# Block B's projection: weight parts from copies in PSUM, x's sums begun in block A, loads ahead of V moved

## The chip, the cores and the metric

The kernel runs on one core of one Trainium2 chip. A core has a matrix engine (PE), which multiplies and adds up in PSUM, eight banks of 128 partitions by 512 numbers; a vector engine (DVE) and an activation engine (ACT), which read and write PSUM and the on-chip memory SBUF; a general engine (POOL), which this kernel uses on SBUF alone; and SyncE (SP), whose queue issues the transfers (DMAs) here. The metric is the device time of one execution in microseconds (us), less is better. Each engine works through its own queue in program order.

## The reference

Two attention blocks of the same sizes, whose results stand side by side in the output: 2048 positions, width 640, 32 heads of 20.

```python
qkv = (x @ wqkv).reshape(B, S, 3, H, Dh)            # both blocks
# block A: each position attends to 8 positions, 2 apart (masked before 0)
logits = einsum("bhsd,bhswd->bhsw", q, kg) * scale
o = einsum("bhsw,bhswd->bhsd", softmax(logits), vg)
# block B: full attention
scores = einsum("bhqd,bhkd->bhqk", q, k) * Dh ** -0.5
o = einsum("bhqk,bhkd->bhqd", softmax(scores), v)
out = concatenate([oA @ woA, oB @ woB], axis=-1)
```

## The kernel before, in words

**Products in parts.** Every fp32 operand is split into a high part (`act.copy` to a rounded type) and a low part (raw minus high, `lo_of`, a `tensor_tensor` subtraction on DVE). A product of 128 rows by 512 columns over one block of 128 takes three matmuls (`PASSES`: high by high, high by low, low by high).

**Stages.** First block A's q, k, v projection for 12 of 16 row tiles (`a_steps`, line 825, driven by the loop at line 862, steps n = 0 to 47). Then block B's q and k projection, 40 groups g0 to g39 (`groups_b`, line 1059, driven by the loop at line 1076). Then block B's v projection, the V stage (line 1664), in groups too, with the first maxima of block B's scores beside it from the seventh group on. Then the attention loop, 512 steps for block B with block A's rest beside it, and the output products.

**Block B's groups.** The 1280 columns of q and k go by ten chunks of 128, taken in pairs, five `WFour` objects WF0 to WF4 (line 768); x goes by four column blocks n of 512. For n = 3 and 2 a pair is multiplied plainly (`b_plain`, line 1048: four groups of 15 matmuls). For n = 0 and 1 the pair and the two blocks of x are multiplied as a two by two scheme with seven products in place of eight (`b_four`, line 1015: four groups of 27, 15, 9 and 3 matmuls). It needs sums of weight blocks (`WFour.sums`) and of x blocks (`XFour.sums`, line 714), and the high and low parts of both: `base` makes the parts of the blocks as they are, `second` those of the sums. The order is: plain WF0 (g0 to g3), plain WF1 (g4 to g7), fours WF0 (g8 to g11) and WF1 (g12 to g15), plain WF2, four WF2, plain WF3, four WF3, four WF4, plain WF4 (g36 to g39). The k columns come first in that order, the q columns after.

**Order of the work.** It is written out by hand. After each group the table `jobs` (line 1067) adds loads, parts and sums to the queues. x's sums run on POOL; WF0's and WF1's weight sums on POOL, the others on DVE; all in place in SBUF. A group's result is evicted by `b_parts` (line 1004): ACT writes the high part into an SBUF tile `pr` from a ring of three, and the low part is put off: `low` (line 999), called in a later group, subtracts on DVE and issues the store on SP. Banks are taken in turn from all eight (`next_bank`, line 446). Block A's attention runs on POOL from g9 on: `a_fetch` (line 537) loads a unit's keys or values into one of two buffers `akv`, and a step of `a_attention` (line 639) is a unit of POOL work. `b_keys` and `b_queries` (lines 969 and 979) load K and q of the first head group for the maxima; `wide_pieces` (line 220) loads v's weights and puts their parts off by `wait[0]` ticks, a tick being a group. A tile taken from a ring waits for all users of its predecessor in that place. Most instructions are recorded by a helper at line 61 (`InOrder`), so the profile gives that line for all of them, and they are told apart by tile: `w` weight parts, `xn`, `xs` and `xl` x's parts, `stg` raw loads, `pr` outputs, `ps_st` PSUM, `bk` and `bq` K and q for attention, `akv` block A's keys and values.

## Time and profile before

| | |
|---|---|
| median of 3 runs | 1759.67 us (1758.86 to 1764.15) |
| the profiled execution | 1763.64 us, span 1761.8 us |
| busy share of the span | PE 98%, DVE 86%, ACT 77%, POOL 72% |
| block B's projection | 147.5 to 298.5 us |
| V stage to the loop | 298.5 to 400.5 us |

A row of the timeline gives the start and the length of a run of like instructions in us, the engine, the operation, output and inputs by tile, their shape and count, and in brackets how long the engine idled before and what ended that. A row of the groups gives total and mean time, then the idle time. A row of the stretches gives the length, each engine's busy time and count (PE, PEld for weight loads, DVE, ACT, POOL; PE alone where only PE was asked for), then the clock granted to PE, the share of DMA time and GB/s.

### The profile page before, as it was taken

What the parts mean: (1) busy time and instruction counts of PE and PEld (TensorE: products, weight loads), DVE (VectorE), ACT (ScalarE), POOL (GpSimd) and SP (SyncE); (2) the same over time, 40 slices, a digit from 0 to 9 for tenths busy, and PEclk for the clock granted to TensorE, in tenths of its full rate; (3) what the DMA queues carried; (4) which work ended last, traced back from release to release, by engine and by line L of the source; (5) the groups of instructions that cost most, each with busy time, mean ns of one, the idle gap of its engine ahead of it and who ended that gap; (6) DMA issues with size and microseconds to landing.
All of it is one profiled execution on the core that took longest, in us unless ns stands there. A gap on an engine that the chain in (4) does not pass through costs nothing.

```text
span 1761.8 us, 32264 instructions
## 1 busy us (share of the span) xinstructions
PE 1731.3 (98%) x11193; PEld 980.3 (56%) x11193; DVE 1517.2 (86%) x2110; ACT 1350.4 (77%) x2639; POOL 1270.7 (72%) x1154
## 2 busy tenths in 40 slices
PE   9999899899999999999999999999999999999999
PEld 8887678775444444444444444445444444444458
DVE  7757574589999999999999999999999999999656
ACT  5224233118999899999999999998999999989882
POOL 0003687395888888888998888988888988868324
PEclk9999899999999999999999999999999999999999
DMA  7667578784445563644464446535553534231223
GB/s 238 221 203 253 199 269 276 223 262 115 142 133 150 138 173 117 165 150 130 139 172 150 139 130 163 161 115 157 136 177 98 137 108 131 80 106 46 58 79 116
DMA packets 224411, 271.20 MB, mean 154 GB/s; under 512 B 92908, under 2 KB 147448, under 8 KB 224248
## 3 DMA queue, kind: packets, MB, share of 16 engines
q1 hardware_dynamic: 223672, 268.49, 51.7%
q8 instruction: 88, 1.44, 0.4%
q14 instruction: 75, 0.61, 0.1%
q10 hardware_dynamic: 576, 0.66, 0.1%
HBM read 194.31 MB, written 74.74 MB: 153 GB/s over the span
## 4 chain that ended last, share of the span: by engine, by line
PE 87%; DVE 4%; DMA 3%; POOL 2%; ACT 1%; issue 1%; SPq 0%; DVEq 0%; POOLq 0%; ACTq 0%
PE ps_st L61 87%; DVE mx L61 2%; DMA bk<-kb_d 1%; ACT e L61 1%; DMA stg<-wqk_b 1%; DVE stg L61 1%; POOL xo L61 1%; DVE w L61 1%; DMA stg<-wv_b 0%; POOL braw L61 0%; POOL xr L61 0%; DMA wr<-xa 0%; POOL stg L61 0%; DMA stg<-xb 0%; SPq L61 0%
## 5 line engine op out<-in xcount | busy, mean ns | idle before, releaser
L61 DVE TENSOR_REDUCE mx<-ps_st 128x1 f32<-128x512 f32 (+1 forms) x1500 | 1218.3, 879 | 79.8 <-PE ps_st L61 68.7
L61 ACT ACTIVATE e<-ps_st 128x512 f32<-128x512 f32 x2048 | 1067.2, 609 | 45.6 <-PE ps_st L61 24.4
L61 PE MATMUL ps_st<-bq,bk 62*128 62x512 f32 x2048 | 612.8, 439 | 0.2
L61 PE MATMUL ps_st<-bk,bq 60*128 60x512 f32 x2048 | 558.1, 435 | 7.2 <-DMA bq<-qb_d 6.0
L61 PEld LDWEIGHTS ps_st<-bq,bk 62*128 62x128 f32 x2048 | 287.4, 184 | 480.6 <-ACT e L61 337.4
L61 PE MATMUL ps_st<-e,vb 128*32 128x512 f32 x4096 | 542.9, 604 | 2.0
L61 POOL TENSOR_TENSOR braw<-braw,more 128x512 f32<-128x512 f32 x224 | 287.7, 1284 | 127.5 <-ACT more L61 119.8
L61 POOL TENSOR_TENSOR akv<-akv 128x640 f32<-128x640 f32 (+3 forms) x304 | 283.4, 932 | 23.8
L61 PEld LDWEIGHTS ps_st<-bk,bq 60*128 60x128 f32 x2048 | 265.7, 184 | 40.6 <-DVE mx L61 12.0
L61 POOL TENSOR_TENSOR akv<-akv,aq 128x1280 f32<-128x1280 f32 x64 | 188.5, 2945 | 28.0 <-DMA akv<-ka_d 28.0
L61 PEld LDWEIGHTS ps_st<-e,vb 128*32 128x32 f32 x4096 | 82.0, 108 | 156.2 <-issue 71.1
L61 POOL TENSOR_TENSOR akv<-akv,al 128x1280 f32<-128x1280 f32 x64 | 151.6, 2369 | 2.3 <-DMA akv<-va_d 2.2
L61 POOL TENSOR_TENSOR stg<-stg 128x512 f32<-128x512 f32 (+1 forms) x16 | 21.1, 1320 | 161.0 <-DVE xs L61 156.8
L61 PE MATMUL ps_st<-wc,xn 128*128 128x512 f32 (+1 forms) x544 | 133.4, 377 | 0.1
L61 ACT COPY more<-ps_st 128x512 f32<-128x512 f32 x224 | 132.5, 591 | 0.7 <-PE ps_st L61 0.4
L61 ACT COPY ro<-ps_st 128x320 f32<-128x320 f32 (+2 forms) x76 | 34.7, 460 | 106.0 <-PE ps_st L61 80.8
L61 PEld LDWEIGHTS ps_st<-wc,xn 128*128 128x128 f32 x544 | 102.1, 188 | 15.1 <-ACT xn L61 0.5
L61 PE MATMUL ps_st<-xn,w 128*128 128x512 f32 x360 | 92.0, 404 | 8.8 <-DVE ps_st L61 4.3
L61 PEld LDWEIGHTS ps_st<-xn,w 128*128 128x128 f32 x360 | 70.2, 196 | 25.4 <-DVE ps_st L61 4.7
L61 ACT CAST pr<-ps_st 128x512 fp32r<-128x512 f32 x40 | 23.4, 587 | 76.3 <-PE ps_st L61 52.0
L61 PE MATMUL ps_st<-ww,aot 128*128 128x320 f32 x480 | 77.8, 314 | 1.7
L61 POOL TENSOR_TENSOR ao<-ao,akv 128x640 f32<-128x640 f32 x48 | 74.8, 1558 | 3.8
(116 smaller groups left out, 1393.3 us busy)
## 6 DMA issues: line engine op xcount, KB each, us to landing
akv<-ka_d SPq DMA_DIRECT2D x128, 320.0 KB
akv<-va_d SPq DMA_DIRECT2D x128, 320.0 KB
wx<-wa_d SPq DMA_DIRECT2D x24, 480.0 KB
kb_d<-pr SPq DMA_DIRECT2D x20, 512.0 KB
qb_d<-pr SPq DMA_DIRECT2D x20, 512.0 KB
bk<-kb_d SPq DMA_DIRECT2D x16, 640.0 KB
bq<-qb_d SPq DMA_DIRECT2D x64, 160.0 KB
rb<-s_d SPq DMA_DIRECT2D x128, 64.0 KB
```

The costliest lines, as they stand in the source:

```text
L61: return self.tc.keep_in_program_order(op(*a, **k))
```

## The change

Block B's weight parts and sums take their operands from PSUM: `lift` lets ACT copy the raw weight blocks into two banks, DVE's sums have one operand there and write their results c and d to banks, and the high and low parts are made from them. WF0 keeps its first parts as they were (`base(False)`). WF0's and WF1's sums leave POOL for DVE. Two or three banks are kept for this (`block_of`), so the groups no longer turn through all eight: g0 takes bank 6, g1 to g7 turn through 0, 1, 2, and from g8 on five banks, 0 to 4, are dealt out by `order_b`. The parts of the last x blocks (`ends`) are subtracted on POOL. Of x's first pair the end parts and half of its sums are made in the last step of block A, and WF1's loads go out in the step before; the rest of x's sums and parts is spread otherwise over jobs 0 to 6. Every fourth output goes to a pair of tiles of another tag (`rb`), stored by two DMAs. v's weight pieces, K's and q's loads are issued earlier; two of block A's fetches move behind g39 to V groups 3 and 5.

```diff
@@ -718,39 +718,46 @@
...
-        def parts(self, hi, lo, src):
+        def parts(self, hi, lo, src, e=dve):
             act.copy(hi, src)
-            lo_of(lo, src, hi)
+            e.tensor_tensor(lo, src, hi.bitcast(F32), ALU.subtract)
+
+        def ends_of(self, kp):
+            self.e.append([p_tile([128, 2, 512], F32R, "xs", "px") for _ in range(3)] if kp else
+                          [sb.tile([128, 2, 512], F32R, tag=tag, bufs=b, name="xs")
+                           for tag, b in (("aot", 1), ("akx", 2), ("akx", 2))])
+            e = self.e[kp][0]
+            self.parts(e[:, 0], e[:, 1], self.raw[kp][1][:, 1])
...
                 self.u = [big(n, [128, 2, KC - 1, 512], "xn") for n in range(2)]
-                self.e.append([sb.tile([128, 2, 512], F32R, tag=tag, bufs=b, name="xs")
-                               for tag, b in (("aot", 1), ("akx", 2), ("akx", 2))])
-            else:
-                self.e.append([p_tile([128, 2, 512], F32R, "xs", "px") for _ in range(3)])
-            u, e = self.u[0][:, :, 2 * kp:2 * kp + 2], self.e[kp][0]
+            u = self.u[0][:, :, 2 * kp:2 * kp + 2]
             self.parts(u[:, 0], u[:, 1], self.raw[kp][0])
-            self.parts(e[:, 0], e[:, 1], self.raw[kp][1][:, 1])
...
                 t = sb.tile([128, 2, 512], F32R, tag="last0", bufs=2, name="xl")
-                self.parts(t[:, 0], t[:, 1], r)
+                self.parts(t[:, 0], t[:, 1], r, gp)
                 self.l.append(lambda i, t=t: t[:, i])
-        def sums(self, kp):
+        def sums(self, kp, part):
             a, b = self.raw[kp]
-            pool(b[:, 1], b[:, 1], b[:, 0], ALU.subtract)
-            pool(b[:, 0], b[:, 0], a[:, 0], ALU.subtract)
+            if not part:
+                pool(b[:, 1], b[:, 1], b[:, 0], ALU.subtract)
+                pool(b[:, 0], b[:, 0], a[:, 0], ALU.subtract)
+                return
             pool(a[:, 0], b[:, 1], a[:, 0], ALU.add)
...
             self.parts(u[:, 0], u[:, 1], self.raw[kp][0])
-            for n in range(2):
+            for n in range(2 - kp):
                 self.parts(e[n + 1][:, 0], e[n + 1][:, 1], self.raw[kp][1][:, n])
+
+        def third(self):
+            self.parts(self.e[1][2][:, 0], self.e[1][2][:, 1], self.raw[1][1][:, 1])
...
@@ -769,7 +776,7 @@
...
         def __init__(self, m, tag, bufs):
-            self.m = MS[2 * m:2 * m + 2]
+            self.n, self.m = m, MS[2 * m:2 * m + 2]
             self.raw = [sb.tile([128, KC, 128], F32, tag=tag, bufs=bufs, name="stg") for _ in range(2)]
...
@@ -779,26 +786,53 @@
...
-        def base(self):
+        def block_of(self, n):
+            r = ((3, 4, 4, 5), (6, 7, 4, 5), (6, 7, 5, 5))[min(self.n, 2)][n]
+            return bank_b(r).rearrange("p (k c) -> p k c", c=128)
+
+        def lift(self):
+
+            self.s = [self.block_of(n) for n in range(2)]
+            for t, r in zip(self.s, self.raw):
+                act.copy(t, r[:, :KC - 1])
+
+        def base(self, lift=True):
             self.x, self.y = (sb.tile([128, 2, KC + 1, 128], F32R, tag="w", bufs=4, name="w") for _ in range(2))
             a, b = self.raw
-            self.parts(self.x, 0, a)
-            self.parts(self.y, 0, b[:, :KC - 1])
-            self.parts(self.x, KC, b[:, KC - 1:])
-
-        def sums(self, e):
-            a, b = ([t[:, o:KC - 1:2] for o in range(2)] for t in self.raw)
-            e.tensor_tensor(b[1], b[0], b[1], ALU.add)
-            e.tensor_tensor(b[0], a[0], b[0], ALU.subtract)
-            e.tensor_tensor(a[0], b[1], a[0], ALU.subtract)
-            e.tensor_tensor(a[1], a[1], a[0], ALU.subtract)
+            if not lift:
+                self.parts(self.x, 0, a)
+                self.parts(self.y, 0, b[:, :KC - 1])
+                self.parts(self.x, KC, b[:, KC - 1:])
+                return
+            self.lift()
+            t = self.block_of(2)[:, :2]
+            for o in range(2):
+                act.copy(t[:, o:o + 1], self.raw[o][:, KC - 1:])
+            self.lows = [(self.x[:, :, :KC - 1], self.s[0]), (self.y[:, :, :KC - 1], self.s[1]), (self.x[:, :, KC - 1:], t)]
+            for u, t in self.lows:
+                act.copy(u[:, 0], t)
+
+        def lo(self):
+            for u, t in self.lows:
+                lo_of(u[:, 1], t, u[:, 0])
+
+        def sums(self):
+            (A, B), (a, b) = self.s, self.raw
+            c, d = self.block_of(3), A
+            ev, od = slice(0, KC - 1, 2), slice(1, KC - 1, 2)
+            for r, x, y, op in ((c[:, od], B[:, ev], b[:, od], ALU.add), (c[:, ev], A[:, ev], b[:, ev], ALU.subtract),
+                                (d[:, ev], c[:, od], a[:, ev], ALU.subtract), (d[:, od], a[:, od], d[:, ev], ALU.subtract)):
+                dve.tensor_tensor(r, x, y, op)
+            self.c, self.d = c, d
         def second(self):
-            a, b = self.raw
             self.z = sb.tile([128, 2, KC + 1, 128], F32R, tag="vb", bufs=2, name="w")
-            self.parts(self.z, 0, a[:, :KC - 1])
-            self.parts(self.y, KC - 1, b[:, :2])
-            self.parts(self.z, KC - 1, b[:, 2:KC - 1])
+            uses = ((self.z, 0, self.d), (self.y, KC - 1, self.c[:, :2]), (self.z, KC - 1, self.c[:, 2:]))
+            uses = [(u[:, :, k:k + t.shape[1]], t) for u, k, t in uses]
+            for u, t in uses:
+                act.copy(u[:, 0], t)
+            for u, t in reversed(uses):
+                lo_of(u[:, 1], t, u[:, 0])
...
@@ -944,8 +978,11 @@
...
             ends_x.append(r)
+            if n == 47:
+                XW.ends_of(0)
+                XW.sums(0, 0)
         if n == 45:
-            WF[0].base()
+            WF[0].base(False)
         elif n == 46:
...
@@ -954,6 +991,8 @@
...
             raw_x.append(r)
+            if n == 46:
+                WF.append(WFour(1, "stg", 3))
     XB[2] = columns(2)
...
@@ -994,7 +1033,11 @@
...
-    lows, last = [], [False]
+    lows, last, outs_p, whole = [], [False], [0], set()
+    order_b, first_b = [6, 0, 1, 2], turn_of[0]
+
+    def bank_b(n):
+        return psb[:, (first_b + n) % 8]
...
@@ -1004,12 +1047,21 @@
...
         o = (0, 1) if c < KC else (1, 0)
-        pt = p_tile([128, 2, 512], F32R, "pr", None if last[0] else "p")
-        act.copy(pt[:, o[0]], p)
+        outs_p[0] += 1
+        d = dst_b(c, n)
+        if last[0] or outs_p[0] % 4:
+            pt = p_tile([128, 2, 512], F32R, "pr", None if last[0] else "p")
+            stores = [(d.rearrange("t p c -> p t c"), pt)]
+            pt = [pt[:, t] for t in range(2)]
+        else:
+            pt = [sb.tile([128, 512], F32R, tag="rb", bufs=2, name="pr") for _ in range(2)]
+            stores = [(d[t], pt[t]) for t in range(2)]
+        act.copy(pt[o[0]], p)
         def lo():
-            lo_of(pt[:, o[1]], p, pt[:, o[0]])
-            sp.dma_start(dst_b(c, n).rearrange("t p c -> p t c"), pt.bitcast(F32))
+            lo_of(pt[o[1]], p, pt[o[0]])
+            for r, t in stores:
+                sp.dma_start(r, t.bitcast(F32))
         lows.append(lo)
...
@@ -1019,7 +1071,10 @@
...
         m = w.m
-        b = [next_bank() for _ in range(4)]
+        b, order_b[:] = order_b[:4], [order_b[n] for n in (4, 0, 3, 2, 1)]
+        assert whole.issuperset(b[2:])
+        whole.update(b)
+        b = [bank_b(b[n]) for n in (0, 2, 1, 3)]
         c = sb.tile([128, 512], F32, tag="raw", bufs=2, name="sum")
...
@@ -1049,7 +1104,10 @@
...
             for j in range(2):
-                p = next_bank()
+                n_b = order_b.pop(0)
+                order_b.append(n_b)
+                whole.add(n_b)
+                p = bank_b(n_b)
                 product(p, [w.block(j, k) for k in range(KC)],
...
@@ -1064,14 +1122,15 @@
...
-    jobs = {0: (kp1, lambda: WF.append(WFour(1, "stg", 3))), 1: (lambda: XW.base(0),),
-            2: (lambda: XW.sums(0), lambda: WF[1].base()),
-            3: (lambda: XW.base(1), lambda: XW.sums(1), lambda: WF[0].sums(gp), lambda: XW.ends([ends_x[1][:, o] for o in range(2)])),
-            4: (lambda: XW.second(0),), 5: (lambda: XW.second(1), lambda: WF[1].sums(gp)), 6: (lambda: WF[0].second(),),
-            7: (lambda: a_fetch(0), lambda: a_fetch(1)), 8: (lambda: WF[1].second(),)}
-    for m, at in ((2, (10, 13, 16, 18)), (3, (18, 21, 23, 24)), (4, (24, 26, 27, 29))):
-        for g, fn in zip(at, (lambda m=m: WF.append(WFour(m, "stg", 3)), lambda m=m: WF[m].base(),
-                              lambda m=m: WF[m].sums(dve), lambda m=m: WF[m].second())):
+    jobs = {0: (kp1, lambda: WF[0].lift(), low, lambda: WF[0].sums(), lambda: XW.base(0), lambda: XW.sums(0, 1)),
+            1: (low, lambda: WF[1].base(), lambda: WF[1].lo()),
+            2: (low, lambda: XW.ends_of(1), lambda: XW.sums(1, 0), lambda: XW.base(1), lambda: XW.sums(1, 1)),
+            3: (lambda: XW.second(0),), 4: (lambda: XW.ends([ends_x[1][:, o] for o in range(2)]),),
+            5: (lambda: XW.second(1),), 6: (lambda: WF[0].second(), lambda: XW.third()),
+            7: (lambda: a_fetch(0), lambda: a_fetch(1)), 8: (lambda: WF[1].sums(),), 9: (lambda: WF[1].second(),)}
+    for m, at in ((2, (9, 12, 13, 16, 18)), (3, (17, 20, 21, 23, 24)), (4, (24, 26, 26, 27, 29))):
+        for g, fn in zip(at, (lambda m=m: WF.append(WFour(m, "stg", 3)), lambda m=m: WF[m].base(), lambda m=m: WF[m].lo(),
+                              lambda m=m: WF[m].sums(), lambda m=m: WF[m].second())):
             jobs[g] = (*jobs.get(g, ()), fn)
...
@@ -1080,23 +1139,25 @@
...
         last[0] = groups > 34
-        if groups == 33:
+        if not groups:
+            order_b.remove(6)
+        elif groups == 7:
+            order_b[:] = [3, 4] + order_b
+        if groups == 30:
             WV, loads = wide_pieces(wv_b[0])
-        elif groups == 38:
-            wait[0] = 4
+        elif groups == 36:
+            wait[0] = 6
             w1, more = wide_pieces(wv_b[1])
...
                 fn()
-        if groups > 35:
-            if groups == 36:
-                k_loads = b_keys(0)
-                rings.append(big(1, [128, NQC, 2, 512], "bq"))
-                q_loads = [fn for qc in range(NQC) for fn in b_queries(0, qc)]
-            k_loads.pop(0)()
-            if groups > 37:
-                for _ in range(2):
-                    q_loads.pop(0)()
-        if groups in (12, 13, 17, 19, 20, 24, 26, 28, 29, 32, 36, 38):
+        if groups == 33:
+            k_loads = b_keys(0)
+        elif groups == 36:
+            rings.append(big(1, [128, NQC, 2, 512], "bq"))
+            q_loads = [fn for qc in range(NQC) for fn in b_queries(0, qc)]
+        if groups > 32:
+            (k_loads if k_loads else q_loads).pop(0)()
+        if groups in (12, 13, 17, 19, 20, 24, 26, 28, 29, 32):
             a_fetch(fetches.pop(0))
...
@@ -1106,7 +1167,7 @@
...
     narrow[0] = False
-    free.append(free.pop(0))
+    free[:] = [b for b in ((first_b + n) % 8 for n in [5, 6, 7] + order_b) if b < 4]
     ones = [sb.tile([128, 16 * VC + 11], F32, tag=tag, bufs=2, name="ve") for tag in ("raw", "rb", "raw", "rb")]
...
@@ -1670,6 +1731,8 @@
...
             wait[0] = 5
+        if fetches and groups in (3, 5):
+            a_fetch(fetches.pop(0))
         if groups in (8, 16):
```

## The prediction

> **What bounds the kernel now.** First the view by stretches: block B's projection (groups g0 to g39), the V stage with the first maxima, and the attention loop.
>
> ```profile
> core 0 of [0], span 1761.8 us
> core 0: us, PE busy (x) PEld busy (x) DVE busy (x) ACT busy (x) POOL busy (x), PEclk, DMA share, GB/s
> 147.48:298.50 151.02, 137.65 (x572) 110.88 (x570) 98.77 (x112) 52.92 (x96) 102.85 (x88) 0.95 0.70 240
> 298.50:400.55 102.05, 95.11 (x582) 80.04 (x581) 65.54 (x66) 22.75 (x46) 70.33 (x58) 0.97 0.80 243
> 400.55:1700.00 1299.45, 1294.90 (x8973) 613.28 (x8972) 1222.36 (x1702) 1195.02 (x2345) 1071.83 (x961) 1.00 0.46 130
> ```
>
> In the loop PE is busy 1294.90 of 1299.45 us, and the change leaves it alone. What can be won lies in the first two rows, where PE idles and the clock is below 1. How much? The groups of PE's matmuls in g0 to g39 give their count, and the timeline of PE the pace and the holes:
>
> ```profile
> L61 PE MATMUL ps_st<-xn,w 128*128 128x512 f32 x360 | 92.0, 404 | 8.8 <-DVE ps_st L61 4.3 <-ACT ps_st L61 2.6 <-DVE w L61 1.4
> L61 PE MATMUL ps_st<-xl,w 128*128 128x512 f32 x120 | 34.3, 402 | 0.0
> L61 PE MATMUL ps_st<-xs,w 128*128 128x512 f32 x90 | 23.6, 407 | 4.6 <-ACT w L61 2.7 <-DVE ps_st L61 1.1 <-DVE w L61 0.8
> ```
> ```profile
> 154.52 2.88 PE L61 MATMUL ps_st<-xn,w 128*128 128x512 f32 x12
> ...
> 157.92 2.88 PE L61 MATMUL ps_st<-xn,w 128*128 128x512 f32 x12
> ...
> 181.68 0.50 PE L61 MATMUL ps_st<-xs,w 128*128 128x512 f32 x1 [2.72 <-ACT w L61]
> ...
> 198.40 2.11 PE L61 MATMUL ps_st<-xn,w 128*128 128x512 f32 x6 [4.30 <-DVE ps_st L61]
> ...
> 314.13 0.46 PE L61 MATMUL ps_st<-bk,bq 60*128 60x512 f32 x1
> 320.55 1.19 PE L61 MATMUL ps_st<-bk,bq 60*128 60x512 f32 x3 [5.96 <-DMA bq<-qb_d]
> ...
> 325.87 0.73 PE L61 MATMUL ps_st<-bk,bq 60*128 60x512 f32 x4
> ...
> 328.93 0.73 PE L61 MATMUL ps_st<-bk,bq 60*128 60x512 f32 x4
> ```
>
> g2 starts at 154.52 and g3 at 157.92: 15 matmuls in 3.40 us, 0.227 each. The 360 + 120 + 90 = 570 matmuls would take 129.2 us; the stage takes 151.0. **21.8 us** are holes and what follows them. In the V stage the sets of four maxima are 328.93 - 325.87 = 3.06 us apart, the first and second 325.87 - 314.13 = 11.74: **8.7 us** more. A hole costs more than its length, as the clock by stretches of 3.41 us shows:
>
> ```profile
> 178.93:182.34 3.41, 0.53 (x2) 1.00 0.21 81
> 182.34:189.17 6.83, 6.21 (x15) 0.50 0.69 217
> 192.58:196.00 3.42, 1.53 (x7) 1.00 0.37 144
> 196.00:199.41 3.41, 1.01 (x4) 1.00 0.00 0
> ```
>
> The stretch with PE busy 0.53 us, in which the 2.72 us hole lies, is followed by half clock (1.7 us of work lost in every 3.41); the one with 1.53 is followed by full clock.
>
> Why do the holes come? The releasers are DVE and ACT making weight parts. DVE's groups, first over the stage, then from 150.5 to 161.5 us, nearly all of it before POOL works:
>
> ```profile
> L61 DVE TENSOR_TENSOR pr<-ps_st,pr 128x512 fp32r<-128x512 f32 x39 | 25.8, 680 | 7.1 <-ACT pr L61 7.1
> L61 DVE TENSOR_TENSOR stg<-stg 128x256 f32<-128x256 f32 x12 | 18.0, 1503 | 0.3
> L61 DVE TENSOR_TENSOR w<-stg,w 128x512 fp32r<-128x512 f32 x9 | 11.7, 1295 | 5.9 <-ACT w L61 5.9
> ```
> ```profile
> L61 DVE TENSOR_TENSOR xn<-stg,xn 128x1024 fp32r<-128x1024 f32 x3 | 3.7, 1224 | 2.4 <-ACT xn L61 2.3
> L61 DVE TENSOR_TENSOR xl<-stg,xl 128x512 fp32r<-128x512 f32 x2 | 1.4, 688 | 1.9 <-ACT xl L61 1.9
> ```
>
> 512 elements with an operand in PSUM take 0.68 us throughout, with both in SBUF 0.69 alone and 1.30 on the mean. The three w subtractions before the hole at 198.40, beside POOL:
>
> ```profile
> 191.91 5.83 DVE L61 TENSOR_TENSOR w<-stg,w 128x512 fp32r<-128x512 f32 x3 [3.08 <-ACT w L61]
> ```
> ```profile
> 191.58 2.94 POOL L61 TENSOR_TENSOR akv<-akv,aq 128x1280 f32<-128x1280 f32 x1 [7.22 <-DMA akv<-ka_d]
> 194.60 3.85 POOL L61 TENSOR_TENSOR akv<-akv 128x640 f32<-128x640 f32 x4
> 198.53 0.32 POOL L61 TENSOR_TENSOR al<-akv 128x64 f32<-128x64 f32 x1
> ```
>
> They end at 197.74, as long as POOL's chain does: each waits for a POOL operation.
>
> **The change, part by part.** *Weight parts and sums from PSUM.* All 12 sums on DVE (18.0 us), the 8 that POOL did for WF0 and WF1, and the low parts of WF1 to WF4 and of every `second` get one operand in PSUM. At the first row's 0.68 for 512 (about 0.42 for 256, by the scale of an uncontended operation) a `sums` is 1.7 us, a `lo` or `second` 1.6, whatever POOL does. So the fours' weights are ready about 3 us after they are asked for, and I remove the holes from g12 on, that at 198.40 among them, whole. The price is ACT's:
>
> ```profile
> L61 ACT COPY ps_st<-ps_st 128x512 f32<-128x512 f32 x5 | 2.9, 583 | 1.0 <-PE ps_st L61 1.0
> ```
>
> two copies of 512 and two of 128 per four, at most 4 x 0.58 = 2.3 us, five times, 11.7 us. ACT is busy 52.92 of 151.02, which hides them; without the cover a copy ahead of an eviction would cost 0.58.
>
> *The banks.* The weights hold three banks, so g0 to g7 turn through three where they had eight: g6 cannot start until DVE has taken the low part of g3. That puts DVE's queue on PE's path in the first eight groups. Its ledger starts here:
>
> ```profile
> 152.98 1.23 DVE L61 TENSOR_TENSOR xn<-stg,xn 128x1024 fp32r<-128x1024 f32 x1 [1.74 <-ACT xn L61]
> ```
>
> Before the low part of g3 stand five subtractions of 1024 (x's: 5 x 1.14, as starts follow 0.08 before the last end), four of 512 from SBUF (x's ends: 2.4), WF0's sums 1.7, WF1's `lo` 1.6, and the low parts of g0 to g3, 2.4: 13.8 us, and 0.7 of waiting for ACT, so 167.5. g6 is due at 154.52 + 4 x 3.40 = 168.1. Alone it would just do. But x's sums on POOL run meanwhile:
>
> ```profile
> L61 POOL TENSOR_TENSOR stg<-stg 128x512 f32<-128x512 f32 x8 | 12.6, 1576 | 160.5 <-DVE xs L61 156.8 <-PE ps_st L61 3.2
> ```
>
> 1.58 with DVE's share in it, some 1.2 once the way is free. `sums(0, 0)` now falls on XB[2]'s parts (1.0 us of waits; 0.45 reaches g2), the four of kp 1 on `second(0)`, three subtractions that each wait for one (3.4). The low part of g3 then ends near 171.7; g6 waits 3.1 us, and its stretch is nearly empty, so 1.7 at half clock: **5.3 us stay** with the 0.45. Bounds: 0 (no waits on POOL) and 13.7 (all eight of POOL's operations, 12.6 us, stand in DVE's way: 180.1, 12.0 after g6 is due, and the clock). I take 5.3, the value by the order in which the operations are written. The first four starts in bank 3, where WF0's sums d lie: its `second` ends about 180, when PE comes at 180.2, so nothing is added.
>
> The Trainium skill ("TensorE: Matmul & The Clock Gate", "Architectural detail" and "HAM oscillation") asks for gaps above about 3.4 us before the clock falls. By that rule g6's 3.1 us would not halve it, and the sum would keep 3.6 instead of 5.3; the trace, where 2.72 us idle was followed by half clock, decides against it.
>
> *x's sums in block A.* `ends_of(0)` and two POOL operations move about 7 us ahead; on ACT and DVE they fall into idle time (1.74 before the row at 152.98). WF1's two loads pass x's ends and kp 1 on SP, which idles there; WF1 is then there for g4, which now waits for its weights (part of the 21.8). kp 1 comes behind them by so much.
>
> *Four homes.* Every fourth output leaves in two DMAs from tag rb: nine more issues on SP, which mostly waits. A home returns after four groups, 12.2 us at the least (one four, 54 x 0.227), where three gave 8.8 (39 matmuls).
>
> *a_fetch and SP.* Ten fetches of block A's keys and values stay where they were in groups, but the groups come sooner, while a unit on POOL takes 198.85 - 191.58 = 7.3 us. A fetch waits on SP for a unit to free its buffer, and stores stand behind it:
>
> ```profile
> SPq L61 <- POOL al L61: 9.9, 3, 6.8
> ```
>
> I reckon waits of 3 to 5 us at g20, g26 and g28; the next store is due only about then, and the homes have 12. I take 1 us for the whole middle (bounds 0 and 7).
>
> *Loads ahead of V.* wv pieces come three groups earlier, K's four loads at g33 to g36 in place of g36 to g39, three of the first four q loads at g37 to g39, and two fetches go behind them, to V groups 3 and 5. Now K's last piece waits on SP until 306.73 and the chain runs over it:
>
> ```profile
> 306.73 12.86 DMA bk<-kb_d
> ```
>
> g39 will end near 283.2 (298.5 - 15.5), the first maxima are due 7 groups or 15.6 us later (314.13 - 298.50), at 298.8. K's last issue stands behind the low part of g35, near 271, and with 12.86 lands at 284. The fourth q load, after g39's store, goes near 285 and would land at 297.9 even if it took 12.86 too, still ahead: I take the 8.7 as gone (bounds 0 and 8.7). What is late next is DVE's maxima at their own pace, as before.
>
> *Sum.* 21.8 + 8.7 - 5.3 - 1.0 = 24.2 us. The profiled execution took 1763.64 (span 1761.8 and 1.8 around it): 1739.4. The median of the runs is 4.0 lower, 1759.67, so **1735.5**.
>
> **The rivals.**
> *A: nothing stays in g0 to g7.* If the copies and POOL interleave kindly, g6 waits under 1.5 us and keeps its clock: 5 more, 1730.5. For it: DVE's plain sum ends at 167.5. Against: five waits on POOL are in the order itself.
> *B: the wait at the first maxima only moves.* The DMA share is 0.70 and 0.80 in the two stretches, and the same bytes must pass in 16 us less. If q still lands last, the 8.7 stays: 1744.2. For it: 306.73's 12.86. Against: two fetches fewer ahead of it, and K's last issue 12 us before V's start in place of 8 behind it.
> *C: POOL paces the middle.* Units contended at 9 us instead of 7.3, over eight scores, would make the late fetches hold SP some 14 us longer than reckoned; beyond the homes' slack that is about 10 us lost: 1746 to 1750.
> *D: given back.* POOL's 70.33 us in the V stage include x's parts and units that PE needs before the loop; if POOL comes to V as late as now, PE waits there what it won: 1759. Against: POOL loses 8 operations, and idles over a quarter of both stretches.
> *E: slower, by stores behind fetches.* If a fetch held for 6.8 us keeps stores back past the homes' 12.2, ACT stops at the next eviction, the turn of five banks is soon full, and PE stops with a halved clock: 6.8 + 1.7 = 8.5 us a time. From four of the ten on it is slower than before by over 5; five give 1735.5 + 42.5 = 1778. Against: it needs late stores and a full turn each time.
>
> **How the numbers follow.** Forecast 0.49, A 0.13, B 0.17, C 0.07, D 0.07, E 0.07. 0.3% is 5.3 us, about what a measurement of this kernel can tell from no change. Faster is the forecast with A, B and C, 0.86; same is D, 0.07; slower E, 0.07. The range runs from A with 2 us to spare, 1728.5, to past C, 1752; D, E and the tails stay out.
>
> **What would show it.** Right: no PE hole over 1 us from g9 to g39, `w` and `s` subtractions at 0.68 beside POOL, one hole of 2 to 4 us at g6 released by DVE's pr, half clock after it, g39's end near 283, no wait on bq. Wrong: PE waiting in the fours on ps_st or on pr's stores (C, E), a bq wait of over 3 us (B), or a loop longer than 1299.45 (D).

## The result, and the profile after

The changed kernel takes **1741.20 us** (median of four runs, 1739.06 to 1743.03); the kernel before, run beside it, took 1759.26 (four runs, 1758.01 to 1764.15). The ratio is 0.9892, with a 95% interval of 0.9870 to 0.9914: faster by 18.1 us. The profiled execution, the fastest of the four, took 1739.06 us with a span of 1737.3.

The view by stretches of the changed kernel, cut as before near the starts of block B's projection, the V stage and the loop, here 0.3 to 0.8 us ahead of them (columns: the stretch, its length, busy time and count of PE, PEld, DVE, ACT and POOL, then PE's clock, the DMA share and GB/s):

```profile
core 0 of [0], span 1737.3 us
147.48:280.50 133.02, 129.87 (x571) 106.55 (x570) 74.97 (x119) 58.46 (x114) 93.55 (x77) 1.00 0.79 274
280.50:376.00 95.50, 94.58 (x597) 79.51 (x595) 65.73 (x67) 23.48 (x48) 72.39 (x65) 1.00 0.83 259
376.00:1677.00 1301.00, 1294.41 (x8973) 613.48 (x8972) 1222.86 (x1704) 1194.77 (x2344) 1073.08 (x960) 1.00 0.46 130
```

PE is now busy for 129.87 of the 133.02 us of the projection, at a clock of 1.00 where it was 0.95. DVE's work there has fallen from 98.77 to 74.97 us, POOL's from 102.85 to 93.55, and ACT's has grown from 52.92 to 58.46. The groups of PE's matmuls in that stage say what is left of idle time:

```profile
L61 PE MATMUL ps_st<-xn,w 128*128 128x512 f32 x360 | 88.0, 390 | 3.1 <-DVE pr L61 2.6 <-DVE xn L61 0.5
L61 PE MATMUL ps_st<-xl,w 128*128 128x512 f32 x120 | 32.9, 389 | 0.0
L61 PE MATMUL ps_st<-xs,w 128*128 128x512 f32 x90 | 22.0, 389 | 0.0
```

The waits on ps_st and on the weight parts `w` are gone. Two holes remain, 0.5 and 2.6 us, and PE's timeline gives their places and the stage's two ends:

```profile
148.06 2.91 PE L61 MATMUL ps_st<-xn,w 128*128 128x512 f32 x12
...
154.89 2.12 PE L61 MATMUL ps_st<-xn,w 128*128 128x512 f32 x8
157.54 1.20 PE L61 MATMUL ps_st<-xn,w 128*128 128x512 f32 x4 [0.53 <-DVE xn L61]
...
159.27 2.89 PE L61 MATMUL ps_st<-xn,w 128*128 128x512 f32 x12
...
172.31 3.02 PE L61 MATMUL ps_st<-xn,w 128*128 128x512 f32 x12 [2.62 <-DVE pr L61]
...
281.26 1.92 PE L61 MATMUL ps_st<-ww,xn 128*128 128x320 f32 x12
...
296.75 0.73 PE L61 MATMUL ps_st<-bk,bq 60*128 60x512 f32 x4
...
299.81 0.73 PE L61 MATMUL ps_st<-bk,bq 60*128 60x512 f32 x4
```

g3 comes 159.27 - 154.89 = 4.38 us after g2, 0.98 more than the 3.40 of a group. g6 is due three groups after g3, at 169.47, and comes at 172.31, 2.84 late. So the stage, from 148.06 to 281.26, takes 133.20: 129.4 of work and 3.8 of waiting. The first and second sets of maxima are 3.06 us apart, where they were 11.74: nothing waits for q.

Cut at the same events in each trace (the first matmul of g0, of the V stage, and the first and last on `e,vb` in the loop), the two profiled executions compare like this:

| us | block A | block B's projection | V stage | loop | span |
|---|---|---|---|---|---|
| before | 147.48 | 151.02 | 103.83 | 1316.19 | 1761.8 |
| after | 148.06 | 133.20 | 95.01 | 1317.70 | 1737.3 |
| gain | -0.6 | 17.8 | 8.8 | -1.5 | 24.5 |

### The profile page after: what moved, and what is told of

Same layout as the page of the kernel before. It is cut to its first block, busy times and chain, and to the rows that moved or that the text cites. A ratio compares the mean times of both kernels' runs of the same rounds, so it can differ in the third digit from the quotient of the medians.

```text
span 1737.3 us, 32288 instructions
## 1 busy us (share of the span) xinstructions
PE 1721.1 (99%) x11193; PEld 974.5 (56%) x11193; DVE 1492.0 (86%) x2116; ACT 1356.0 (78%) x2657; POOL 1263.5 (73%) x1148
## 4 chain that ended last, share of the span: by engine, by line
PE 89%; DVE 3%; POOL 2%; ACT 2%; DMA 1%; issue 1%; SPq 1%; DVEq 0%; POOLq 0%; ACTq 0%
PE ps_st L61 89%; DVE mx L61 2%; ACT e L61 1%; POOL braw L61 1%; POOL xo L61 1%; SPq L61 1%; DMA va_d<-ro 0%; POOL xr L61 0%; DMA stg<-wo_a 0%; DMA stg<-xb 0%; ACT more L61 0%; POOL aot L61 0%; DVE xs L61 0%; DMA qa_d<-ro 0%; DVE xn L61 0%
## 5 line engine op out<-in xcount | busy, mean ns | idle before, releaser
L61 POOL TENSOR_TENSOR stg<-stg 128x512 f32<-128x512 f32 x8 | 13.6, 1694 | 156.9 <-DVE xs L61 149.8
L61 PE MATMUL ps_st<-xn,w 128*128 128x512 f32 x360 | 88.0, 390 | 3.1 <-DVE pr L61 2.6
L61 POOL TENSOR_TENSOR braw<-braw,rb 128x512 f32<-128x512 f32 x32 | 41.3, 1290 | 49.1 <-DMA rb<-s_d 39.1
```

The lines of the kernel that those rows point to most:

```text
L61: return self.tc.keep_in_program_order(op(*a, **k))
```

## The experiments

A stage length below is always taken at these events. "The changed kernel" alone means the profiled execution above. The kernel before, run beside each, took 1761.76 us beside the two experiments on g6, the one without copies and the one with the old loads; 1760.21 beside the changed kernel again, the three homes and the first two of the better orders; and 1761.02 beside the rest.

**The two kernels again.** Does what the traces show repeat?

> The changed kernel once more, beside the variants. Theory (executions differ by where the clock's stretches of 3.41 us fall on the same holes): its runs spread over 1739 to 1744, the granted clock lower by 0.001 for each 1.7 us, with the hole at g6 between 2 and 3 us in a second trace too. Rival (the trace shown was another course of events): holes at other places, times unrelated to the clock.

The changed kernel took 1743.27 us (1742.44 to 1745.77), ratio 0.9907 (0.9890 to 0.9923). Its timeline has the same two holes and nothing else up to the V stage:

```profile
158.01 1.18 PE L61 MATMUL ps_st<-xn,w 128*128 128x512 f32 x4 [0.52 <-DVE xn L61]
...
172.78 4.37 PE L61 MATMUL ps_st<-xn,w 128*128 128x512 f32 x12 [2.63 <-DVE pr L61]
```

But after the hole the twelve matmuls take 4.37 us where they took 3.02. The stretches of 3.41 us show why, first in this execution, then in the one above:

```profile
170.70:174.12 3.42, 1.34 (x6) 1.12 (x7) 2.62 (x3) 0.90 (x2) 3.34 (x3) 1.00 0.16 59
174.12:177.54 3.42, 3.42 (x10) 2.65 (x9) 3.17 (x3) 0.73 (x2) 2.61 (x2) 0.50 0.66 247
```
```profile
170.64:174.05 3.41, 1.74 (x8) 1.44 (x9) 2.36 (x4) 1.23 (x2) 3.33 (x4) 1.00 0.27 100
174.05:177.46 3.41, 3.41 (x17) 2.83 (x16) 3.38 (x3) 1.75 (x5) 2.23 (x1) 1.00 0.55 208
```

The hole is equally long, but PE was busy 1.34 us of the one stretch and 1.74 of the other: the first is followed by half clock, the second is not. The stage takes 135.33 here and 133.20 there.

> The kernel before once more, for a second trace. Theory (its executions share the waits and differ by the halved clock): the same waits in the stage, 148 to 151 us for the stage, and a loop of 1317.3 us as in all variants, so that the 1316.2 of the trace shown was chance. Rival (the change makes the loop longer): a loop of 1316.2 again.

The kernel before took 1757.87 us in this one execution. Its projection takes 145.81 us where the first trace had 151.02, its V stage 102.89, its loop 1316.78. Six of the seven holes of the first trace come again. In place of the 4.30 us at 198.40 there is this one:

```profile
209.17 2.79 PE L61 MATMUL ps_st<-xn,w 128*128 128x512 f32 x11 [1.04 <-DVE w L61]
```

So the 21.8 us of holes and half clock in the trace on which the prediction rests belong to that execution; this one has 145.81 - 129.2 = 16.6, and its stage is shorter than the 148 to 151 that were expected. The length of the loop falls between the two expectations; a hole in it tells them apart (see the rivals below).

**What makes g6 wait?** The prediction's answer is the queue of DVE, lengthened by waits on POOL. First the low part of g3 is put ahead of `second(0)`:

```diff
-            3: (lambda: XW.second(0),), 4: (...),
+            3: (low, lambda: XW.second(0)), 4: (...),
```

> The low part of g3 is subtracted ahead of x's second(0). Theory (DVE's queue behind POOL's x sums sets the pace of the first eight groups): the hole of 2.6 us at g6 goes, but second(1) still waits for POOL's sums, WF0's second part ends near 179 us, and about 3 us of hole comes back ahead of the first four (g8): the stage ends within 1 us of the changed kernel's 281.3. Rival (the late low part is the whole of it): no new hole, the stage ends 2.5 to 3 us sooner.

1738.63 us (1737.83 to 1741.05), ratio 0.9876 (0.9858 to 0.9893). g6 no longer waits, and the first four does:

```profile
178.50 1.66 PE L61 MATMUL ps_st<-xn,w 128*128 128x512 f32 x6 [2.33 <-DVE w L61]
```

The projection takes 132.87, as before the edit. The hole moved by the order of DVE's queue: the lateness belongs to the queue as a whole, not to one place in it. (The median is 2.6 us under the changed kernel's along with less half clock: three of these four executions show a mean clock of 1.0, three of the changed kernel's four 0.998.) Then the suspected cause is taken away, POOL's four operations of x's second pair; this kernel leaves those sums out and multiplies the blocks as they are:

```diff
-            2: (low, lambda: XW.ends_of(1), lambda: XW.sums(1, 0), lambda: XW.base(1), lambda: XW.sums(1, 1)),
+            2: (low, lambda: XW.ends_of(1), lambda: XW.base(1)),
```

> x's sums of the second pair on POOL are left out, so the fours multiply unsummed blocks. Theory (DVE waits for POOL's operations one by one): DVE's second(0), at 2.3, 1.8 and 1.8 us in the changed kernel, takes 1.2, 0.7 and 0.7; the low part of g3 ends near 169; g6 waits under 0.5 us, the first four is not late either, and the stage ends about 2.8 us sooner. Rival (DVE's queue is too long by itself with three banks): the hole at g6 stays over 2 us.

1736.67 us (1736.30 to 1738.19), ratio 0.9863 (0.9848 to 0.9878); the projection takes 130.19. Neither g6 nor the first four waits. The subtractions of `base(1)` (the first of 1024) and `second(0)` and the low parts behind them on DVE, in the changed kernel and here, with POOL's row of the changed kernel between:

```profile
164.84 3.46 DVE L61 TENSOR_TENSOR xn<-stg,xn 128x1024 fp32r<-128x1024 f32 x2
168.21 3.44 DVE L61 TENSOR_TENSOR xs<-stg,xs 128x512 fp32r<-128x512 f32 x2
171.58 1.27 DVE L61 TENSOR_TENSOR pr<-ps_st,pr 128x512 fp32r<-128x512 f32 x2
```
```profile
165.05 7.74 POOL L61 TENSOR_TENSOR stg<-stg 128x512 f32<-128x512 f32 x4 [0.68 <-issue]
```
```profile
163.97 2.35 DVE L61 TENSOR_TENSOR xn<-stg,xn 128x1024 fp32r<-128x1024 f32 x2
166.24 1.28 DVE L61 TENSOR_TENSOR xs<-stg,xs 128x512 fp32r<-128x512 f32 x2
167.44 1.28 DVE L61 TENSOR_TENSOR pr<-ps_st,pr 128x512 fp32r<-128x512 f32 x2
```

With both operands in SBUF the two pairs take 3.46 and 3.44 us beside POOL's four operations, 2.35 and 1.28 without them: 3.3 us more, somewhat above the 2.84 by which g6 is late. Two low parts, which have one operand in PSUM, take 1.27 and 1.28 in both. That DVE's queue alone would be too long falls.

**What the operands in PSUM are worth.** All copies are left out, the weight sums and parts are made by DVE from SBUF, and the rest of the change is kept (one load moves from g17 to g18, since its buffer comes free later):

```diff
-            self.s = [self.block_of(n) for n in range(2)]
-            for t, r in zip(self.s, self.raw):
-                act.copy(t, r[:, :KC - 1])
+            self.s = [r[:, :KC - 1] for r in self.raw]
...
-            c, d = self.block_of(3), A
+            c, d = B, A
```

> The changed kernel without the copies: weight parts and sums of all fours are made in SBUF as before, all on DVE, the five banks, the homes and the moved loads kept (WF3's load one group later). Theory (the operand in PSUM is what keeps DVE from waiting for POOL): the w subtractions of 512 come back to 1.2 us or more on the mean, the sums to 1.5 each, holes return in the fours, and the stage is 8 us longer (4 to 14). Rival (the other order and the loads bring the gain): within 2 us of the changed kernel.

1754.44 us (1749.37 to 1755.62), ratio 0.9954 (0.9939 to 0.9968): 7.3 us are left of the 18.1 by the medians, each beside its own kernel before, so about 11 are gone, and 10.3 between the profiled executions (1749.37). Its projection takes 141.32, 8.1 more than the changed kernel's. Its three longest holes (the first is that at g6), and DVE's groups over the stage, here and in the changed kernel:

```profile
173.66 3.04 PE L61 MATMUL ps_st<-xn,w 128*128 128x512 f32 x12 [3.56 <-DVE pr L61]
...
254.71 3.04 PE L61 MATMUL ps_st<-xs,w 128*128 128x512 f32 x12 [2.30 <-DVE ps_st L61]
...
265.61 3.02 PE L61 MATMUL ps_st<-xn,w 128*128 128x512 f32 x12 [1.74 <-ACT ps_st L61]
```
```profile
L61 DVE TENSOR_TENSOR stg<-stg 128x256 f32<-128x256 f32 x20 | 14.6, 728 | 0.5
L61 DVE TENSOR_TENSOR w<-stg,w 128x512 fp32r<-128x512 f32 x9 | 12.3, 1363 | 0.0
```
```profile
L61 DVE TENSOR_TENSOR w<-ps_st,w 128x512 fp32r<-128x512 f32 x13 | 8.5, 682 | 4.8 <-ACT w L61 4.7
...
L61 DVE TENSOR_TENSOR ps_st<-ps_st,stg 128x256 f32<-128x256 f32 x15 | 6.4, 429 | 0.3
```

A subtraction of 512 costs 1.36 us from SBUF and 0.68 from PSUM, and the holes around 255 and 265 come back. A sum of 256 costs 0.73 against 0.43, half of the 1.5 that were expected. The Trainium skill ("SBUF — State Buffer", "SBUF: two separate sides") says that a DVE operation with two SBUF inputs and a POOL operation that reads SBUF exclude each other for a whole instruction; the rows of this and the last experiment agree.

**The loads ahead of V.** V's weight pieces, K's and q's loads and two fetches go back to their old groups:

```diff
-        if groups == 33:
-            k_loads = b_keys(0)
-        elif groups == 36:
...
+        if groups > 35:
+            if groups == 36:
+                k_loads = b_keys(0)
```

> The changed kernel with the loads of v's weights, K and q and the two fetches at their old places. Theory (they are late by their place in the queue): the wait on bq at the first maxima is back with 5 to 10 us, half clock included, and the time is 5 to 10 us over the changed kernel's. Rival (they were late behind a stage held up by DVE, and the shorter stage alone cures it): under 2 us.

1749.43 us (1748.52 to 1750.62), ratio 0.9934 (0.9919 to 0.9949). The V stage takes 104.00 where it took 95.01, and the wait is back:

```profile
305.44 1.19 PE L61 MATMUL ps_st<-bk,bq 60*128 60x512 f32 x3 [5.97 <-DMA bq<-qb_d]
```

So the moved loads are worth 9.0 us in the V stage, taken together (which of them does it was not tried), and the shorter projection, which this kernel has too (135.25), does not bring them. By the medians, each beside its own kernel before, 12.3 us are left of 18.1 and 16.9.

**The other parts.** The ends and first sums of x's first pair go back from block A to job 0:

```diff
-            if n == 47:
-                XW.ends_of(0)
-                XW.sums(0, 0)
...
-    jobs = {0: (kp1, lambda: WF[0].lift(), low, lambda: WF[0].sums(), lambda: XW.base(0), lambda: XW.sums(0, 1)),
+    jobs = {0: (kp1, lambda: WF[0].lift(), low, lambda: WF[0].sums(), lambda: XW.ends_of(0), lambda: XW.sums(0, 0), lambda: XW.base(0), lambda: XW.sums(0, 1)),
```

> The changed kernel with the end parts and first sums of x's first pair back in job 0, after g0, in place of block A's last step. Theory (POOL's chain of eight x sums stands in DVE's way in the order of the queues): POOL's sums of the second pair come 2 to 3 us later, the hole at g6 grows to 4 to 6 us, with the clock halved after it, the time is 3 to 5 us over the changed kernel's. Rival (the start in block A only fills idle time): within 1 us.

1745.44 us (1743.77 to 1748.10), ratio 0.9908 (0.9888 to 0.9928). g6 waits 4.79 us where it waited 2.62, half clock follows, and the projection takes 137.66: 2.3 more than in the second trace of the changed kernel, which has half clock there too. So that part of the change pays in the traces; the medians, 15.6 us below the kernel before where the changed kernel is 16.9 and 18.1 below, lie too close to show it. The fourth home of the outputs, instead, is left out like this:

```diff
-        if last[0] or outs_p[0] % 4:
+        if True:
```

> The changed kernel with three homes for the outputs, all in one ring, no second pair of tiles. Theory (with low parts in time a home is back within 9 us): ACT waits a few us more for stores, PE less than 1, the time is within 2 us of the changed kernel's. Rival (the fourth home carries part of the gain): holes in the fours released by ACT's pr or ps_st, 3 us or more.

1741.13 us (1739.16 to 1742.40), ratio 0.9889 (0.9870 to 0.9908). Projection, V stage and loop take 135.38, 95.03 and 1318.76, against 135.33, 95.01 and 1319.08 in the changed kernel's second trace. The fourth home brings nothing that can be seen.

**Why g2 waits longer than reckoned.** It lost 0.98 us, not 0.45. The raw part of x that it waits for came late. SP issues it just ahead of WF1's two loads in the changed kernel:

```profile
149.59 0.39 SPq L61 DMA_DIRECT2D stg<-xb  x1
150.07 0.91 SPq L61 DMA_DIRECT2D stg<-wqk_b  x2
```

ACT's rows show when the part is there, in the changed kernel and then in one in which WF1's two loads are issued a step later, behind x's ends:

```diff
             if n == 47:
                 XW.ends_of(0)
                 XW.sums(0, 0)
+                WF.append(WFour(1, "stg", 3))
...
-            if n == 46:
-                WF.append(WFour(1, "stg", 3))
```

> The changed kernel with WF1's weights loaded one step later, behind x's ends. Theory: x's column block 2 lands sooner, g2's wait falls to 0.5 us, but WF1's weights land about 161 and the wait at g4 that the kernel before had is back with 1 to 3 us. Rival (WF1's place in the queue matters little): no wait at g4.

```profile
155.18 1.05 ACT L61 CAST xn<-stg 128x1024 fp32r<-128x1024 f32 x1 [2.00 <-DMA stg<-xb]
```
```profile
153.75 1.06 ACT L61 CAST xn<-stg 128x1024 fp32r<-128x1024 f32 x1 [0.78 <-DMA stg<-xb]
```

ACT gets the part 1.4 us sooner in the trace, 0.8 sooner counted from the start of g0, and g2 loses only 0.39 (its twelve matmuls take 3.27 us instead of 2.88), because DVE's subtraction for it takes 1.67 us beside POOL where it takes 1.23 alone:

```profile
154.84 1.67 DVE L61 TENSOR_TENSOR xn<-stg,xn 128x1024 fp32r<-128x1024 f32 x1 [0.57 <-ACT xn L61]
```
```profile
154.49 3.27 PE L61 MATMUL ps_st<-xn,w 128*128 128x512 f32 x12
...
162.46 2.79 PE L61 MATMUL ps_st<-xn,w 128*128 128x512 f32 x11 [0.23 <-DVE w L61]
...
171.94 4.60 PE L61 MATMUL ps_st<-xn,w 128*128 128x512 f32 x12 [2.61 <-DVE pr L61]
```

So with the data on time POOL costs g2 about the 0.45 of the prediction. In the changed kernel that subtraction takes 1.23 us, clear of POOL, and the late data make the whole 0.98. That WF1's loads make them late is shown by moving those loads alone; how they slow a part issued 0.5 us before them is not. The second half of the expectation failed: g4, whose weights now come later, waits 0.23 us, not 1 to 3. The one execution took 1740.56 us, with half clock behind g6.

**A better order.** If g6 waits because it needs a bank that DVE has not emptied, a fourth bank helps, and if the first four waits for `WF[0].second`, that can stand earlier. Bank 4 joins the turn after g2, and `WF[0].second` moves from job 6 to job 4:

```diff
-            3: (lambda: XW.second(0),), 4: (lambda: XW.ends([ends_x[1][:, o] for o in range(2)]),),
-            5: (lambda: XW.second(1),), 6: (lambda: WF[0].second(), lambda: XW.third()),
+            3: (lambda: XW.second(0),), 4: (lambda: WF[0].second(), lambda: XW.ends([ends_x[1][:, o] for o in range(2)])),
+            5: (lambda: XW.second(1),), 6: (lambda: XW.third(),),
...
+        elif groups == 2:
+            order_b.insert(1, 4)
         elif groups == 7:
-            order_b[:] = [3, 4] + order_b
+            order_b.insert(0, 3)
```

> The changed kernel with bank 4 taken into the turn of g3 to g7 (four banks in place of three) and WF0's second parts moved from job 6 to job 4. Theory: neither g6 (a bank of four is free a group earlier) nor the first four (bank 3 is read out by 174) waits; the stage ends 2.8 us sooner, the clock is not halved in it, 3 to 5 us less than the changed kernel. Rival (one of the two holes only moves on, as with the low part of g3 taken first): less than 1 us.

1736.48 us (1736.11 to 1736.88), ratio 0.9866 (0.9851 to 0.9881). The holes at g6 and the first four are gone, but g4, the first in bank 4, waits for DVE, as it seems to read WF1's copy out of it, and the stage ends 1.6 us sooner than in the changed kernel's first trace, not 2.8:

```profile
156.51 0.73 PE L61 MATMUL ps_st<-xn,w 128*128 128x512 f32 x2 [0.24 <-ACT xn L61]
157.78 1.20 PE L61 MATMUL ps_st<-xn,w 128*128 128x512 f32 x4 [0.53 <-DVE xn L61]
...
163.97 3.01 PE L61 MATMUL ps_st<-xn,w 128*128 128x512 f32 x12 [0.89 <-DVE w L61]
```

Next, x's second load for g2 goes out a step earlier, together with the first and so well ahead of WF1's weights:

```diff
-        if n in (45, 46):
-            a, b = PAIRS[n - 45]
-            r = p_tile([128, b - a, 512], F32, "stg", "p")
...
-            if n == 46:
-                WF.append(WFour(1, "stg", 3))
+        if n == 45:
+            for a, b in PAIRS[:2]:
...
+        elif n == 46:
+            WF.append(WFour(1, "stg", 3))
```

> As the run before it, and the second load of x's column block 2 goes out with the first, ahead of WF1's weights. Theory (that load came 1.5 us later behind a fuller queue, and made the 1 us at g2): g2 waits under 0.3 us, 0.7 to 1 us less than without. Rival (POOL's first two sums alone make it): no difference.

1735.93 us (1735.20 to 1736.55), ratio 0.9863 (0.9848 to 0.9878); the projection takes 130.96 where the last one took 131.77. g2's wait shrinks less than expected, to 0.45, which is POOL's part. Last, bank 4 serves g5 instead of g4 (`order_b.insert(2, 4)`):

> As the variant with all three edits, but bank 4 enters the turn one place later: g5 takes it, not g4. Theory (g4 waited 0.7 to 0.9 us because WF1's last weight block is read from bank 4 just then): that wait goes, 0.7 us less than with bank 4 at g4. Rival (DVE's queue at g4 is late whatever the bank): the wait stays.

1736.30 us (1735.19 to 1737.30), ratio 0.9853 (0.9832 to 0.9874). The wait at g4 is gone, so it was the bank. One hole is left in the projection, which takes 129.92:

```profile
155.49 2.56 PE L61 MATMUL ps_st<-xn,w 128*128 128x512 f32 x10 [0.40 <-DVE xn L61]
```

The 1.0 us won in the stage cannot be told in the time, since the loop of this execution has a stretch at half clock that the last kernel's had not. All three are faster than both kernels: the first two, run beside the changed kernel, are 6.8 and 7.3 us below its 1743.27 and the runs do not overlap; the third was not run beside it, but its four runs lie below all eight of the changed kernel. Some 2 us of the 6.8 were won in the loop, which these edits were not meant to change (1319.08 in the changed kernel's second trace, 1317.14 in the first of the three).

## Why the prediction was right, and where its sizes were off

**The time.** Forecast were 1735.5 us, and the median came out at 1741.20, 5.7 above. Against its own execution the sum gave 1739.4, and the profiled execution took 1739.06; that they agree to 0.3 us is partly luck. The projection was to give 21.8 - 5.3 - 1.0 = 15.5 us and gave 17.8, and block A and the loop, put at nothing, took 2.1 back. The step that failed is the last one: taking a loss of one execution off the median of the runs. The projection of the kernel before lost 21.8 us in that execution and 16.6 in another, so the median, 4.0 below that execution, did not hold the whole of it. From the second trace of before (1757.87) to the second of after (1742.79) the gain is only 15.1. With the losses of that trace, 16.6 in the projection and 102.89 - 95.01 = 7.9 in the V stage, the prediction's terms give 16.6 + 7.9 - 6.3 = 18.2, and block A and the loop take 3.0 of it.

**Weight parts from PSUM, the middle.** Right: the subtractions take 0.68 us beside POOL, and from g9 to g39 PE has no hole in either trace of the changed kernel. Without the copies holes come back. The 1.0 us kept for the middle and SP's queue came out as 0.

**g6.** Right in place, cause and size. The ledger had the low part of g3 done near 171.7; it ends at 171.58 + 0.68 = 172.26, and the hole is 2.62 us for 3.1. POOL makes DVE's queue 3.3 us longer, for 3.4 reckoned. The mis-sized term is the half clock: 1.7 us were added as certain, and it follows in the second trace and not in the first. Rival A (nothing stays) falls by the hole itself. At the first four nothing was added, rightly, but by a small margin and only because g6 is late. DVE ends WF0's `second` at 177.70 + 1.35 = 179.05, and PE comes at 179.24. With the low part of g3 taken first `second` ends sooner, at 178.44, but PE comes sooner still and waits 2.33.

**g2.** The term 0.45 measured 0.98. That DVE waits for POOL was the right mechanism for the 0.4 seen when the data is on time; missed was that WF1's loads, issued right behind x's part, make it reach ACT about 0.9 us later (7.12 us after g0's start, where the kernel before has 153.72 - 147.48 = 6.24). The prediction called SP's queue idle and counted a delay for the loads behind WF1's (kp 1), but not for the part that was already on its way.

**The V stage.** Right: 8.7 forecast, 8.8 found, and 9.0 lost again with the old order. The wait was gone although the DMA share rose from 0.80 to 0.83, so rival B falls. The projection ends at 281.26 for a forecast of 283.2 (283.0 by the prediction's own terms, 298.5 - 15.5).

**The four homes.** The prediction's times until a home is needed again, 12.2 us and 8.8, are not the least. Where a four is followed by a plain pair, four groups are 9 + 3 + 15 + 15 = 42 matmuls, 9.5 us, and three groups of one four are 15 + 9 + 3 = 27, 6.1 us. The run with three homes, which loses nothing, shows that neither mattered.

**Rivals C, D and E.** No hole in the middle speaks for C, and none for E. D's sign, a longer loop, is there in part. (The stretches of 1299.45 and 1301.00 us in the two views do not end at the same events and cannot be compared.) The loop is 1.5 us longer in the first pair of traces, 2.3 in the second. One stretch of 3.41 us at half clock, 1.7 us, makes most of the second (columns as above, from the second trace of the changed kernel):

```profile
1624.80:1628.20 3.40, 1.48 (x9) 0.61 (x7) 3.37 (x6) 2.72 (x6) 1.27 (x1) 1.00 0.70 231
1628.20:1631.60 3.40, 3.40 (x14) 3.07 (x14) 0.74 (x3) 0.00 (x0) 1.70 (x3) 0.50 0.04 7
```

With such stretches taken off, the loops of the changed kernel and its variants take 1316.7 to 1317.9 us, against 1316.2 and 1316.8 in the two traces of before. The changed kernel has one hole near the loop's end, before an output product, that before has not; here are the rows of the changed kernel's two traces:

```profile
1625.97 1.11 PE L61 MATMUL ps_st<-ww,xo 128*128 128x320 f32 x6 [1.93 <-DVE mx L61]
```
```profile
1628.13 1.88 PE L61 MATMUL ps_st<-ww,xo 128*128 128x320 f32 x6 [1.92 <-DVE mx L61]
```

PE waits there for DVE's maxima. In the traces of before the same product, at 1649.83 in the first, does not wait; PE idles 4.5 and 4.8 us in their whole loops, and 6.6 and 6.5 in those of the changed kernel. The stretch with 1.48 us above is the one in which this hole lies, so it brings the half clock too. It is there in every variant but the first two of the better orders, which have 0.5 and 0.3 us in its place. So the step "the change leaves the loop alone" failed by about 1 us, and by 1.7 more where half clock follows. Why the change makes that product wait stays open, as does the cause of the 0.6 us by which block A ended later (over all variants it ends between 147.3 and 148.1, so that may be chance). D's wait for POOL, which would eat all that was won, is not there.

## What to carry to other kernels

Where DVE and POOL read SBUF at the same time, count for each DVE operation with two SBUF operands up to one POOL operation of waiting (3.3 us over three subtractions here), and let an idle ACT copy one operand to PSUM if a bank can be spared; then ask whose bank it was, since a shorter turn of banks puts the evicting engine on PE's path. Read a loss from at least two executions before it is taken off a median: holes and half clock differ from one to the next. When a load is moved forward, look at the row that waits for the transfer issued just before it, not only at what the queue issues behind it.

## What the runs showed of the hardware that was not expected

The same hole, 2.62 and 2.63 us, costs its own length in one execution and 1.7 us more in another. The stretches of 3.41 us lie otherwise over the work each time, and PE's busy time in one stretch goes with what follows. Of the stretches at full clock in the projections of all traces, those with up to 1.34 us busy are followed by half clock, and those with 1.53 (in the trace of before) and more, 1.74 among them, are not; in the loop 1.48 us are followed by it. So the border lies near 1.5 of 3.41 in these rows. It is not the whole rule: in the loop of the kernel without copies, 2.21 us busy (from 1629.38 to 1632.79) are followed by half clock, while 2.18 (from 1629.26 to 1632.67) in the kernel with x's first sums back in job 0 are not. What tells these two apart stays open.

The Trainium skill ("TensorE: Matmul & The Clock Gate", "What's actually happening") says that the window is free-running, with which these rows agree. The rule of gaps above about 3.4 us in the Trainium skill ("HAM oscillation"; its section "Architectural detail", which the prediction names as well, does not have it) is too mild for this kernel, where the hole of 1.92 us in the loop suffices.
